# q and k loaded by token parity, so that one transpose takes two heads and one copy takes 128 partitions; epsilons added from a constant tile

## The chip, the cores and the metric

The kernel runs on 1 core of one Trainium2 chip. The metric is the device time of one execution in microseconds (us). Engines are called by the profile's names: PE (matrix multiply), PEld (its weight loads), DVE (vector), ACT (scalar), POOL (GpSimd), SP (the queue that issues nearly all DMAs here).

## What is computed

Three layers follow each other. Only the first one is touched by the layout part of the change; the epsilons stand in the first and the second.

```python
def _attn_ref(q, k, v):               # 4 batches, 8 heads, 576 tokens, 64 dims; chunks of 64 tokens
    scores = scale * np.matmul(q_c, k_c.transpose(0, 1, 2, 4, 3))
    scores = scores - np.max(scores, axis=-1, keepdims=True)
    attn = np.exp(scores)
    attn = attn / (np.sum(attn, axis=-1, keepdims=True) + 1e-09)
    out = np.matmul(attn, v_c)
...
def _moe_ref(x, w_gate, w1, w2):      # x: 2304 tokens x 512; 8 experts, 1024 hidden
    logits = x @ w_gate
    P = np.exp(logits - logits.max())
    for _ in range(8):
        P /= P.sum(1, keepdims=True) + 1e-09
        P /= P.sum(0, keepdims=True) + 1e-09
        P *= N / E
    for e in range(E):
        h = np.maximum(x @ w1[e], 0.0)
        out += P[:, e:e + 1] * (h @ w2[e])
...
def _moe2_ref(x, w_in, w_out, g_ln):  # SoLU, layer norm and a second product, 512 -> 1024 -> 512
```

All tensors are float32.

## The kernel before

**Stages.** The attention fills the first 110 us or so. Then come the expert products (split into high and low parts and arranged as a seven-product block scheme), which fill most of the time, with the eight Sinkhorn rounds (`sink_rows`, `sink_cols`) beside the first of them. The last layer stands at the end.

**The attention loop.** The 2304 tokens are cut into 18 tiles of 128 tokens (two chunks). The main loop runs over steps `s` and is software-pipelined by hand: at step `s` the program writes, in this order, the loads of the q and k that steps `s+4` and `s+5` transpose (`load_qk`, every second step), the load of v for tile `s-2` (`load_v`, four DMAs), the exponentials and sums of tile `s-3` (`attn_exp`), the product with v of tile `s-6` (`attn_pv`), the transposes of the probabilities of tile `s-5` (`attn_pt`), the scores of tile `s-2` (`attn_qk`) and the transposes of q or k (`attn_t(s)`: q at even steps, k at odd ones; one q and one k tile serve two tiles of tokens). Behind these, queues of small pieces of work are drained (`side`, `w_side`): splitting the attention's output into high and low parts (`x_hi` on ACT, `x_lo` mostly on POOL) and preparing expert weights (`w_steps`, on POOL and ACT). Each engine works its instructions off in the order in which they are written, so a wait on one instruction holds all that is behind it on that engine.

**DMAs.** SP issues the loads and the stores in program order. A DMA also waits until the DMA eight places ahead of it has landed. v of tile `s-2` is loaded at step `s` and read at step `s+4`. q, k and the prepared weights share one pool of 18 buffers, v and the weights' sums another of 6.

**The transposes of q and k (`attn_t`).** A row of the loaded q tile is a pair of neighbouring tokens of one head, so 128 partitions hold 128 pairs of tokens, and a row has 4 heads x 128 numbers (token 0's 64 dims, then token 1's). One 128x128 transpose thus takes one head with both tokens: the result in PSUM has the even tokens in the upper 64 partitions and the odd ones in the lower 64. The tile wanted, `qkt`, has two heads in its 128 partitions and the tokens in order. So each of the two PSUM banks (one for the even heads, one for the odd heads) is copied out in two pieces of 64 partitions:

```python
if t == 0 or (h and not i):
    nc.scalar.activation(out=to, in_=of, func=AF.Copy)
else:
    nc.vector.tensor_copy(to, of)
```

That is four copies of 64x512 for each tile: three on ACT and one on DVE for q, two on each for k. There are 9 q tiles and 9 k tiles.

**The epsilons.** In `attn_exp` (18 times), `sink_rows` (8) and `sink_cols` (8) the epsilon is added to a row of sums by a DVE `tensor_scalar` with an immediate.

Of the kernel before, what the change touches and what calls it, by code (L numbers as in the profile page):

```python
# [9 lines left out]
F32 = mybir.dt.float32  # L10
F32R = mybir.dt.float32r
U32 = mybir.dt.uint32
AF = mybir.ActivationFunctionType
ALU = mybir.AluOpType
# [30 lines left out]
def chunk_attention_sinkhorn_moe_solu_kernel(  # L45
# [13 lines left out]
    nc = tc.nc  # L59
    P = 128  # L60
    B, H, S, D = q.shape
    N, DM = out.shape
    E = w_gate.shape[1]
    F = w1.shape[2]
    NT = N // P
    KD = DM // P
    NP = H // 2
# [4 lines left out]
    EPS = 1e-9  # L72
# [18 lines left out]
    def unit(m):  # L91
        p, i = divmod(m, NU)
        return p, ORDER[p][i]
# [3 lines left out]
    for m in range(NM):  # L97
        p, u = unit(m)
# [4 lines left out]
    const = ctx.enter_context(tc.tile_pool(name="const", bufs=1))  # L103
# [6 lines left out]
    def bank(name):  # L110
        return ps.tile([P, 512], F32, tag="r", name=name)
# [11 lines left out]
    def four(shape, dt, name):  # L123
        return work.tile(shape, dt, tag="four", bufs=4, name=name)
# [10 lines left out]
    def wtile(shape, dt, name):  # L135
        return work.tile(shape, dt, tag="w", bufs=18, name=name)

    ident = const.tile([P, P], F32, name="ident")
    ones = const.tile([P, P], F32, name="ones")
    mhalf = const.tile([P, 1], F32, name="mhalf")  # L140
    g_sb = const.tile([P, KF], F32, name="g_sb")
    wg_raw = const.tile([P, KD, E], F32, name="wg_raw")

# [10 lines left out]
    qk, vs = {}, {}  # L154

    def load_qk(g):

        for i, src in enumerate((q, k)):
            qk[g, i] = [wtile([P, NP, 2 * D], F32, f"{'qk'[i]}{g}_{x}") for x in range(2)]
            done = 0  # L160
            while done < P:
                b, s = divmod(g * P + done, S // 2)
                n = min(P - done, S // 2 - s)
                for x in range(2):
                    nc.sync.dma_start(
                        out=qk[g, i][x][done:done + n],
                        in_=src[b, x * NP:(x + 1) * NP, 2 * s:2 * (s + n), :].rearrange(
                            "h (p t) d -> p h (t d)", t=2
                        ),
                    )  # L170
                done += n
# [13 lines left out]
    def attn_t(s):  # L185


        g, i = divmod(s, 2)
        a = qk.pop((g, i))
        qkt[g, i] = four([P, NP, 4, 64], F32, f"{'qk'[i]}t{g}")  # L190
        o = qkt[g, i].rearrange("p a c (x t) -> p a c t x", t=2)
        for h in range(2):
            pqk = bank(f"pqk{s}_{h}")
            for n in range(NP):
                x, y = divmod(2 * n + h, NP)
                nc.tensor.transpose(pqk[:, n * P:(n + 1) * P], a[x][:, y, :], ident)
            for t in range(2):
                to = o[h * 64:(h + 1) * 64, :, :, t, :]
                of = pqk[t * 64:(t + 1) * 64].rearrange("p (a c x) -> p a c x", a=NP, c=4)
                if t == 0 or (h and not i):  # L200
                    nc.scalar.activation(out=to, in_=of, func=AF.Copy)
                else:
                    nc.vector.tensor_copy(to, of)  # L203

    def attn_qk(t):

# [29 lines left out]
    def attn_exp(t):  # L236
        p, sm = attn[t]
        flat = p.rearrange("p a h x -> p (a h x)")
        heads = p.rearrange("p a h x -> p (a h) x")
        nc.scalar.activation(out=flat, in_=flat, func=AF.Exp, scale=SCALE)  # L240
        nc.vector.tensor_reduce(out=sm, in_=heads, axis=AX.X, op=ALU.add)
        nc.vector.tensor_scalar(out=sm, in0=sm, scalar1=EPS, scalar2=None, op0=ALU.add)
        nc.vector.reciprocal(out=sm, in_=sm)
        nc.gpsimd.tensor_tensor(
            out=heads, in0=heads, in1=sm.unsqueeze(2).to_broadcast([P, H, 64]), op=ALU.mult
        )
# [151 lines left out]
    def sink_rows():  # L398
        r = small.tile([P, NT], F32, tag="sr", name="sr")
        nc.vector.tensor_reduce(out=r, in_=pw, axis=AX.X, op=ALU.add)  # L400
        nc.vector.tensor_scalar(out=r, in0=r, scalar1=EPS, scalar2=None, op0=ALU.add)
        nc.vector.reciprocal(out=r, in_=r)
        nc.vector.tensor_tensor(
            out=pw, in0=pw, in1=r.unsqueeze(2).to_broadcast([P, NT, E]), op=ALU.mult
        )
# [8 lines left out]
    def sink_cols(pc):  # L414
        r = small.tile([P, E], F32, tag="sc", name="sc")
        nc.vector.tensor_reduce(
            out=r, in_=pc[:, :NT * E].rearrange("p (t e) -> p e t", e=E), axis=AX.X, op=ALU.add
        )
        nc.vector.tensor_scalar(out=r, in0=r, scalar1=EPS, scalar2=None, op0=ALU.add)
        nc.vector.reciprocal(out=r, in_=r)  # L420
        nc.vector.scalar_tensor_tensor(
            out=pw,
            in0=pw,
            scalar=float(N) / E,
            in1=r.unsqueeze(1).to_broadcast([P, NT, E]),
            op0=ALU.mult,
            op1=ALU.mult,
        )
# [88 lines left out]
    def w_steps(u):  # L517

        s = {}
        ts = nc.gpsimd.tensor_tensor  # L520

        def a(i, kh):
            return raws[u, 0][kh].rearrange("p (k i f) -> p k i f", k=2, i=2)[:, :, i, :]

        def tmp(n):
            i = ("S1", "S2", "S3", "S4").index(n)
            if i % 2 == 0:
                s["t", i // 2] = vtile([P, 2, 2, P], F32, f"ws{u}_{i}")
            s[n] = s["t", i // 2][:, i % 2]
            return s[n]  # L530

        def put(n, src):
            t = wtile([P, 2, 2, P], F32R, f"w{u}_{n}")
            split(t[:, 0], t[:, 1], src, nc.gpsimd)
            wo[u, n] = t
            i = WOPS.index(n)
            nc.sync.dma_start(
                out=w_kept[u][:, i * 512:(i + 1) * 512],
                in_=t.bitcast(F32).rearrange("p s k f -> p (s k f)"),
            )  # L540

        def s12():
            ts(out=tmp("S1"), in0=a(1, 0), in1=a(1, 1), op=ALU.add)
            ts(out=tmp("S2"), in0=s["S1"], in1=a(0, 0), op=ALU.subtract)

        def s34():
            ts(out=tmp("S3"), in0=a(0, 0), in1=a(1, 0), op=ALU.subtract)
            ts(out=tmp("S4"), in0=a(0, 1), in1=s["S2"], op=ALU.subtract)

        return [  # L550
            s12,
            lambda: put("A11", a(0, 0)),
            s34,
            lambda: put("A12", a(0, 1)),
            lambda: put("S2", s["S2"]),
            lambda: put("S3", s["S3"]),
            lambda: put("S1", s["S1"]),
            lambda: put("A22", a(1, 1)),
            lambda: put("S4", s["S4"]),
        ]  # L560
# [10 lines left out]
    def second_blocks(u):  # L571

        def block(n):
            def go():
                t = wtile([P, 2, 256], F32R, f"w2_{u}_{n}")
                split(t[:, 0], t[:, 1], w2_block(u, n), nc.gpsimd)
                wo2[u, n] = t
                if n != "A21" or u in PLAIN:
                    w_keep(u, n, True, t)
            return go  # L580

        return [block(n) for n in ("A11", "A12", "A21", "A22")]
# [508 lines left out]
    with tc.manual_schedule():  # L1091
# [4 lines left out]
            nc.tensor.transpose(warm[:, :P], ident, ident)  # L1096
        nc.gpsimd.memset(ones, 1.0)
        nc.gpsimd.memset(mhalf, -0.5)
        nc.gpsimd.memset(wg.bitcast(F32), 0.0)

        def split_gate():
# [41 lines left out]
        for g in range(AHEAD // 2):  # L1143
            load_qk(g)
        w_side.extend(w_steps(0))
        banks.clear()
        for s in range(NT + 6):
            if s % 2 == 0 and s + AHEAD < NT:
                load_qk((s + AHEAD) // 2)
# [15 lines left out]
            if s == NT:  # L1165
                a, b = w_steps(1), second_blocks(0)
                w_side.extend(a[:4] + b[:2] + a[4:7] + b[2:] + a[7:])
            if 0 <= s - 3 < NT:
                attn_exp(s - 3)
            if 0 <= s - 6 < NT:  # L1170
                attn_pv(s - 6)
                hp, r = divmod(s - 6, TH)
# [6 lines left out]
            if s < NT:  # L1179
                attn_t(s)  # L1180
# [25 lines left out]
        for m in range(NU, M2):  # L1206
# [3 lines left out]
            g = 7 * (NU + 2) + 6 * (m - NU)  # L1210
            event(g, lambda u=u: load_raw(u, (1,)))
            f = second_sums(u, nc.gpsimd, nc.gpsimd)
# [15 lines left out]
        for n in range(NM):  # L1228
            p, u = divmod(n, NU)
# [21 lines left out]
            if n < NU and n in EARLY:  # L1251
                f = second_sums(n, nc.vector, nc.vector)
# [46 lines left out]
        g = 7 * NM  # L1299
# [60 lines left out]
```

## Time and profile before

| what | value |
|---|---|
| timed runs | 1817.41 us median of 3 (1814.68 to 1820.43) |
| profiled execution | its span from the first to the last instruction is 1814.0 us; the page gives no other time of it, and the fastest timed run is 0.7 us longer, the median 3.4 us |
| PE busy | 1761.4 us, 97% of the span |
| PEld busy | 1701.2 us, 94% |
| DVE busy | 1474.2 us, 81% |
| POOL busy | 1050.4 us, 58% |
| ACT busy | 612.5 us, 34% |
| DMA | 313443 packets, 476.21 MB, mean 263 GB/s |

PE is nearly full over the whole span, but not at its start: in 40 slices of 45 us its busy tenths read 7 7 7 9 9 9 and so on, and those of DVE 6 9 5 8 9 9. The first three slices hold the attention and the start of the Sinkhorn rounds. A difference between two kernels that both have a full PE later shows in when that full stretch begins.

### The profile page before, as it was taken

Reading aid. Unit: us, or ns where it says so; the run is one execution under the profiler, and the core shown is the slowest. Engines: PE = TensorE matmul, PEld = TensorE weight load, DVE = VectorE, ACT = ScalarE, POOL = GpSimd, SP = SyncE. Lnnn points to the kernel's source line nnn. Section 1 sums busy time; section 2 is a strip of 40 time slices with the busy share of each in tenths; the row PEclk is TensorE's granted clock in tenths of the full one; section 3 lists DMA queues with packets and bytes.
Section 4 is the critical chain, followed back from the end, with each engine's and each line's share of the span. In section 5 each row is a group of like instructions: output and inputs, shape, how many; then the busy total and the mean of one; then the engine's idle time right before and its main releaser. Section 6 shows DMA issues by size and latency. Waiting matters only on the chain.

```text
span 1814.0 us, 31893 instructions
## 1 busy us (share of the span) xinstructions
PE 1761.4 (97%) x10827; PEld 1701.2 (94%) x10827; DVE 1474.2 (81%) x2264; ACT 612.5 (34%) x1368; POOL 1050.4 (58%) x1111
## 2 busy tenths in 40 slices
PE   7779999999999999999999999999999999999999
PEld 6668999999999999999999999999999999988887
DVE  6958899999889877778888888988888877766664
ACT  6843444444444312222222222222222322222222
POOL 2866799999988415455466665666565665400000
PEclk8999999999999999999999999999999999999999
DMA  7684888988878898998988889888888878931110
GB/s 186 187 289 155 305 280 293 334 317 289 316 288 309 317 352 263 342 350 317 326 301 277 301 282 385 293 279 276 283 286 285 272 256 272 299 139 64 56 47 30
DMA packets 313443, 476.21 MB, mean 263 GB/s; under 512 B 47664, under 2 KB 116416, under 8 KB 313280
## 3 DMA queue, kind: packets, MB, share of 16 engines
q1 hardware_dynamic: 312848, 471.80, 76.1%
q8 instruction: 87, 1.43, 0.3%
q10 hardware_dynamic: 432, 2.36, 0.3%
q14 instruction: 76, 0.62, 0.1%
HBM read 323.51 MB, written 150.54 MB: 261 GB/s over the span
## 4 chain that ended last, share of the span: by engine, by line
PE 84%; DVE 8%; DMA 5%; ACT 1%; issue 1%; POOL 0%; SPq 0%; DVEq 0%; ACTq 0%
PE y L803 20%; PE y L854 17%; PE Y L663 15%; PE X L663 10%; PE Z L663 10%; PE po L1077 5%; PE mh L1020 5%; DMA wl_A<-wk 2%; PE lt L1065 1%; DVE acc L830 1%; DMA wl_S<-wk 1%; DMA x_B<-xk_B 1%; DVE kt L203 1%; DMA xk_B<-x_B 1%; DMA v<-in_v_dram 0%
## 5 line engine op out<-in xcount | busy, mean ns | idle before, releaser
L683 POOL TENSOR_TENSOR ho_T<-hT,ho_T 128x384 fp32r<-128x384 f32 x188 | 211.1, 1124 | 175.9 <-ACT ho_T L682 168.4
L803 PE MATMUL y<-h,w_A 128*128 128x384 f32 x1536 | 304.8, 336 | 1.9 <-DVE acc L830 1.9
L803 PEld LDWEIGHTS y<-h,w_A 128*128 128x128 f32 x1536 | 269.6, 188 | 3.8 <-issue 2.5
L151 POOL TENSOR_TENSOR w_A<-raw,w_A 128x256 fp32r<-128x256 f32 x224 | 190.7, 864 | 73.6 <-ACT w_A L150 61.5
L758 DVE TENSOR_TENSOR t<-Y,s 128x384 f32<-128x384 f32 x192 | 106.1, 553 | 109.2 <-PE Y L663 92.6
L830 DVE TENSOR_TENSOR acc<-y,acc 128x768 f32<-128x768 f32 (+1 forms) x192 | 175.7, 915 | 10.7 <-PE y L803 9.9
L854 PE MATMUL y<-ho_T,wl_S 128*128 128x384 f32 x864 | 173.4, 335 | 0.2 <-DMA wl_S<-wk 0.2
L874 DVE TENSOR_TENSOR acc<-y,acc 128x768 f32<-128x768 f32 (+1 forms) x165 | 150.5, 915 | 17.8 <-PE y L854 17.7
L803 PE MATMUL y<-h,wl_A 128*128 128x384 f32 x768 | 153.3, 337 | 2.0 <-DMA wl_A<-wk 2.0
L663 PE MATMUL X<-x_B,wl_A 128*128 128x384 f32 x768 | 153.7, 334 | 0.0
L663 PE MATMUL Y<-x_T,wl_S 128*128 128x384 f32 x768 | 153.7, 334 | 0.0
L854 PEld LDWEIGHTS y<-ho_T,wl_S 128*128 128x128 f32 x864 | 152.5, 189 | 1.1 <-PE Z L663 0.5
L737 ACT ACTIVATE h<-c 128x384 fp32r<-128x384 f32 x132 | 69.3, 525 | 235.2 <-DVE c L733 226.6
L803 PEld LDWEIGHTS y<-h,wl_A 128*128 128x128 f32 x768 | 136.2, 190 | 2.8 <-ACT h L737 2.6
L682 ACT ACTIVATE ho_B<-c 128x384 fp32r<-128x384 f32 x96 | 50.5, 526 | 252.1 <-DVE c L716 215.4
L663 PEld LDWEIGHTS Y<-x_T,wl_S 128*128 128x128 f32 x768 | 135.0, 188 | 0.0
L663 PEld LDWEIGHTS X<-x_B,wl_A 128*128 128x128 f32 x768 | 135.0, 188 | 0.0
L682 ACT ACTIVATE ho_T<-hT 128x384 fp32r<-128x384 f32 x192 | 98.9, 516 | 105.1 <-POOL hT L691 100.3
L1051 POOL TENSOR_TENSOR r<-r,mhalf 128x1 f32<-128x1 f32 x18 | 9.9, 548 | 208.8 <-DVE r L1048 208.8
L758 DVE TENSOR_TENSOR c<-Z,t 128x384 f32<-128x384 f32 x192 | 105.1, 548 | 21.6 <-PE Z L663 13.8
L151 POOL TENSOR_TENSOR w_S<-ws,w_S 128x256 fp32r<-128x256 f32 x128 | 110.6, 881 | 7.6 <-ACT w_S L150 7.3
L854 PE MATMUL y<-ho_B,wl_A 128*128 128x384 f32 x576 | 114.8, 334 | 0.0
(172 smaller groups left out, 3877.3 us busy)
## 6 DMA issues: line engine op xcount, KB each, us to landing
wl_S<-wk SPq DMA_DIRECT2D x448, 256.0 KB, 5.2
wl_A<-wk SPq DMA_DIRECT2D x400, 256.0 KB, 5.2
wk<-w_S SPq DMA_DIRECT2D x256, 256.0 KB, 5.1
wk<-w_A SPq DMA_DIRECT2D x208, 256.0 KB, 4.5
raw<-in_moe_w_dram SPq DMA_DIRECT2D x77, 512.0 KB, 5.8
sh<-spread SPq DMA_DIRECT2D x64, 192.0 KB, 8.1
kept<-wp SPq DMA_DIRECT2D x32, 256.0 KB, 5.1
xk_T<-x_T SPq DMA_DIRECT2D x8, 768.0 KB, 4.8
```

Source lines behind the costliest of these rows:

```text
L151: (eng or nc.vector).tensor_tensor(out=lo, in0=src, in1=hi.bitcast(F32), op=ALU.subtract)
L663: nc.tensor.matmul(b, w[:, a, kk, :], x[:, c, kk, :], start=(first and kk == 0 and n == 0), stop=(kk == 1 and n == 2), skip_group_check=no ...
L682: nc.scalar.activation(out=hi, in_=x, func=AF.Copy)
L683: f = lambda: eng.tensor_tensor(out=lo, in0=x, in1=hi.bitcast(F32), op=ALU.subtract)
L737: nc.scalar.activation(out=hi, in_=hp, func=AF.Copy)
L758: nc.vector.tensor_tensor(out=c_of[n], in0=bank_, in1=c_of[other], op=ALU.add)
L803: nc.tensor.matmul(y, wo2[u, f"A{d // 2 + 1}{f + 1}"][:, a, i * P:(i + 1) * P], h[:, c, f, :], start=(f == 0 and n == 0), stop=(f == 1 and ...
L830: nc.vector.tensor_tensor(out=at, in0=y, in1=at, op=ALU.add)
L854: nc.tensor.matmul(y, wo2[unit(m + q_)[1], wn][:, a, i * P:(i + 1) * P], hop[m // 2, bn][:, q_, c, :], start=(q_ == 0 and o == 0), stop=(q ...
L874: nc.vector.tensor_tensor(out=at, in0=y, in1=at, op=ALU.add)
L1020: nc.tensor.matmul(ph[:, n * 512:(n + 1) * 512], x[a][:, kk, :], m_in[kk, c][:, n * 512:(n + 1) * 512], start=(kk == 0 and i == 0), stop=( ...
L1077: nc.tensor.matmul(po[t], lt[f // 4][a][:, f % 4, :], m_out[f, c], start=(f == 0 and i == 0), stop=(f == KF - 1 and i == 2),)
```

## The change

Three things are changed.

- `load_qk` lays q and k out as parity, head, dim in each partition (`[P, 2, NP, D]`) where it was head, parity, dim. The bytes are the same; the piece that lies in one run in DRAM and in the tile is now 64 numbers (256 bytes) long where it was 128 (512 bytes). The number of DMAs is the same.
- `attn_t` transposes two neighbouring heads of one parity at a time. The result has the two heads in the 128 partitions already, so each of the two banks (now one for each parity) is copied out by one instruction of 128x512: two on ACT for q, one on ACT and one on DVE for k. The number and size of the transposes are the same.
- The 34 epsilons of attention and Sinkhorn are added by a DVE `tensor_tensor` with a constant tile `eps` that POOL fills once at the start. The line in the last layer (`mlp_n`) stays as it was.

```diff
+    eps = const.tile([P, NT], F32, name="eps")
...
-            qk[g, i] = [wtile([P, NP, 2 * D], F32, f"{'qk'[i]}{g}_{x}") for x in range(2)]
+            qk[g, i] = [wtile([P, 2, NP, D], F32, f"{'qk'[i]}{g}_{x}") for x in range(2)]
...
                         in_=src[b, x * NP:(x + 1) * NP, 2 * s:2 * (s + n), :].rearrange(
-                            "h (p t) d -> p h (t d)", t=2
+                            "h (p t) d -> p t h d", t=2
...
-        for h in range(2):
-            pqk = bank(f"pqk{s}_{h}")
+        for t in range(2):
+            pqk = bank(f"pqk{s}_{t}")
             for n in range(NP):
-                x, y = divmod(2 * n + h, NP)
-                nc.tensor.transpose(pqk[:, n * P:(n + 1) * P], a[x][:, y, :], ident)
-            for t in range(2):
-                to = o[h * 64:(h + 1) * 64, :, :, t, :]
-                of = pqk[t * 64:(t + 1) * 64].rearrange("p (a c x) -> p a c x", a=NP, c=4)
-                if t == 0 or (h and not i):
-                    nc.scalar.activation(out=to, in_=of, func=AF.Copy)
-                else:
-                    nc.vector.tensor_copy(to, of)
+                x, y = divmod(2 * n, NP)
+                nc.tensor.transpose(
+                    pqk[:, n * P:(n + 1) * P],
+                    a[x][:, t, y:y + 2, :].rearrange("p h d -> p (h d)"),
+                    ident,
+                )
+            of = pqk.rearrange("p (a c x) -> p a c x", a=NP, c=4)
+            if t and i:
+                nc.vector.tensor_copy(o[:, :, :, t, :], of)
+            else:
+                nc.scalar.activation(out=o[:, :, :, t, :], in_=of, func=AF.Copy)
...
-        nc.vector.tensor_scalar(out=sm, in0=sm, scalar1=EPS, scalar2=None, op0=ALU.add)
+        nc.vector.tensor_tensor(out=sm, in0=sm, in1=eps[:, :H], op=ALU.add)
...
-        nc.vector.tensor_scalar(out=r, in0=r, scalar1=EPS, scalar2=None, op0=ALU.add)
+        nc.vector.tensor_tensor(out=r, in0=r, in1=eps, op=ALU.add)
...
+        nc.gpsimd.memset(eps, EPS)
```

On DVE, the second and third steps of the attention read as follows before (`s` are the scores, `p` the probabilities, `mx` their maxima, `sm` their sums, `pqk` the PSUM banks of the transposes; the numbers are buffers):

```order
L228 TENSOR_TENSOR p_251<-s_234,mx_252 128x2x4x64
L203 COPY qt_256<-pqk_0_257 64x512
L241 TENSOR_REDUCE sm_253<-p_251 128x8
L242 TENSOR_SCALAR sm_253<-sm_253 128x8
L243 RECIPROCAL sm_253<-sm_253 128x8
L227 TENSOR_REDUCE mx_299<-s_281 128x8
L228 TENSOR_TENSOR p_298<-s_281,mx_299 128x2x4x64
L203 COPY kt_303<-pqk_0_304 64x512
L203 COPY kt_303<-pqk_1_311 64x512
```

After the change the same place has no copy of q, one copy of k, and the epsilon with two inputs:

```order
L231 TENSOR_TENSOR p_249<-s_232,mx_250 128x2x4x64
L244 TENSOR_REDUCE sm_251<-p_249 128x8
L245 TENSOR_TENSOR sm_251<-sm_251,eps 128x8
L246 RECIPROCAL sm_251<-sm_251 128x8
L230 TENSOR_REDUCE mx_295<-s_277 128x8
L231 TENSOR_TENSOR p_294<-s_277,mx_295 128x2x4x64
L204 COPY kt_299<-pqk_1_306 128x512
```

Nothing else changes its place on DVE; over the kernel 18 rows fewer stand there (2230 for 2248), and 9 rows fewer on ACT (1337 for 1346; two neighbouring copies of one bank share a row).

On SP, around the sixth load of q and k, before:

```order
L180 DMA v_381<-in_v_dram 64x4x64 x4
L165 DMA q_0_435<-in_q_dram 128x4x128
L165 DMA q_1_436<-in_q_dram 128x4x128
L165 DMA k_0_439<-in_k_dram 128x4x128
L165 DMA k_1_440<-in_k_dram 128x4x128
L180 DMA v_443<-in_v_dram 64x4x64 x4
L180 DMA v_517<-in_v_dram 64x4x64 x4
```

and after:

```order
L181 DMA v_373<-in_v_dram 64x4x64 x4
L166 DMA q_0_425<-in_q_dram 128x8x64
L166 DMA q_1_426<-in_q_dram 128x8x64
L166 DMA k_0_429<-in_k_dram 128x8x64
L166 DMA k_1_430<-in_k_dram 128x8x64
L181 DMA v_433<-in_v_dram 64x4x64 x4
L181 DMA v_505<-in_v_dram 64x4x64 x4
```

No DMA has moved; SP has 1676 rows in both. Each load of q and k is made of 8 runs of 64 numbers for each partition where it was 4 runs of 128.

## Rows read from the trace of the kernel before

**Rows 1.** Busy time in a window: PE, PEld, DVE, ACT, POOL; clock, DMA share, GB/s.

```profile
60.00:80.00 20.00, 13.62 (x300) 11.41 (x301) 19.07 (x29) 15.38 (x28) 19.92 (x15) 1.00 0.70 187
```

**Rows 2.** Groups by line to 220 us: busy us, mean ns, idle before.

```profile
L201 ACT ACTIVATE qt<-pqk 64x512 f32<-64x512 f32 x27 | 16.9, 625 | 16.2 <-PE pqk L196 15.9
L203 DVE COPY kt<-pqk 64x512 f32<-64x512 f32 x18 | 12.5, 694 | 2.4 <-ACT kt L201 1.9
L242 DVE TENSOR_SCALAR sm<-sm 128x8 f32<-128x8 f32 x18 | 11.0, 613 | 0.6
L256 ACT ACTIVATE pt<-pt 128x512 f32<-128x512 f32 x18 | 10.5, 582 | 0.0
```

**Rows 3.** Chain of work that ended last, steps 2 and 3: start, us, what.

```profile
13.89 0.63 ACT qt L201
...
18.54 0.71 DVE kt L203
```

**Rows 4.** SP's issues in order of time: start, us, line, DMA, count.

```profile
4.11 2.45 SPq L165 DMA_DIRECT2D k<-in_k_dram  x2
...
35.88 1.85 SPq L165 DMA_DIRECT2D q<-in_q_dram  x2
37.82 1.02 SPq L165 DMA_DIRECT2D k<-in_k_dram  x2
38.89 5.90 SPq L180 DMA_DIRECT2D v<-in_v_dram  x8
...
80.07 2.63 SPq L180 DMA_DIRECT2D v<-in_v_dram  x4
```

**Rows 5.** Chain of work that ended last, around 40 us.

```profile
40.19 5.26 DMA v<-in_v_dram
45.50 1.24 PE px L267 x28
```

**Rows 6.** PE in order of time, the product of the thirteenth tile.

```profile
86.09 1.15 PE L267 MATMUL px<-pt,v 64*64 64x64 f32 x32
```

**Rows 7.** SP's issues by line: duration ns min/median/max, first and last start; v's landing.

```profile
L165 SPq DMA_DIRECT2D k<-in_k_dram x2: 499/503/507, 1.8 to 2.3; - x2
L165 SPq DMA_DIRECT2D q<-in_q_dram x4: 614/614/616, 22.9 to 24.8; - x4
L180 SPq DMA_DIRECT2D v<-in_v_dram x72: 595/615/1638, 15.2 to 101.6; - x72
DMA to landing us min/median/max: 2.3/3.1/5.3
L1154 SPq DMA_DIRECT2D g_sb<-in_moe_g_ln_dram x1: 505/505/505, 19.7 to 19.7; - x1
```

**Rows 8.** DMA traffic from 7 to 9, 55 to 57 and 42.5 to 42.8 us.

```profile
DMA packets 1187, 0.59 MB, mean 295 GB/s; under 512 B 36, under 2 KB 1187, under 8 KB 1187
...
q1 hardware_dynamic: 805, 0.19, 43.1%
...
DMA packets 208, 0.05 MB, mean 174 GB/s; under 512 B 199, under 2 KB 208, under 8 KB 208
```

**Rows 9.** DVE and POOL in order of time, one epsilon.

```profile
57.92 1.31 DVE L242 TENSOR_SCALAR sm<-sm 128x8 f32<-128x8 f32 x1
...
55.61 3.59 POOL L301 TENSOR_TENSOR x_B<-xf,x_B 128x768 fp32r<-128x768 f32 x2 [1.28 <-ACT x_B L297]
```

**Rows 10.** DVE and POOL in order of time, a two-input operation of Sinkhorn.

```profile
131.61 0.56 DVE L421 SCALAR_TENSOR_TENSOR pw<-pw,sc 128x144 f32<-128x144 f32 x1
...
131.26 0.75 POOL L151 TENSOR_TENSOR w_A<-raw,w_A 128x256 fp32r<-128x256 f32 x1
```

**Rows 11.** Durations by line on DVE: ns min/median/max, first and last start.

```profile
L242 DVE TENSOR_SCALAR sm<-sm x18: 170/452/1658, 15.9 to 99.7; 128x8 f32<-128x8 f32 x18
...
L421 DVE SCALAR_TENSOR_TENSOR pw<-pw,sc x8: 307/414/562, 131.6 to 168.6; 128x144 f32<-128x144 f32 x8
L1043 DVE TENSOR_TENSOR r<-su x18: 158/159/163, 1603.6 to 1797.9; 128x1 f32<-128x1 f32 x18
```

More of the change, by code (lines that the diff above doesn't have):

```diff
@@ L418, in sink_cols @@
         )
-        nc.vector.tensor_scalar(out=r, in0=r, scalar1=EPS, scalar2=None, op0=ALU.add)
+        nc.vector.tensor_tensor(out=r, in0=r, in1=eps[:, :E], op=ALU.add)
         nc.vector.reciprocal(out=r, in_=r)
```

## Prediction

> **What bounds the kernel now.** I read the busy slices of the page first: PE is full from the fourth slice on, so all that can move lies in the first 110 us or so. A change there moves the end of the kernel one for one, because the expert products wait for the attention's output and then fill PE. Next I read the windows of that stretch. In a typical one of 20 us DVE is busy for 19.07 and POOL for 19.92, PE for only 13.62 [rows 1]: here DVE and POOL look like the bound. The groups by line say what fills DVE and ACT: a copy of 64x512 out of PSUM takes 0.694 us on DVE and 0.625 on ACT [rows 2]. The chain of waits shows both kinds on the path: after the last of ACT's q copies come the exponentials, and after the second of DVE's k copies the scores [rows 3].
>
> Read only so far, removing copies must pay. But the chain also goes through SP's queue. From 35.88 to 44.79 us the rows of SP join almost without gaps, 8.77 us of issuing in 8.91 us [rows 4]. SP isn't waiting for buffers there; it is late with the program. The cost shows at tile 4: one of its v loads is issued at 40.19, lands 5.26 us later, and the product with v starts at 45.50, as soon as it is there [rows 5]. At tile 12 the four loads of v are issued by 82.70 [rows 4]; with the median landing of 3.1 us [rows 7] they are there at 85.8, and the product starts at 86.09 [rows 6]. So the loads of v arrive just in time both early and late in the attention: SP's pace and the pace of DVE, ACT and POOL are nearly equal. The reader should see that the first two views name a bound and the queue's own rows name a second one right behind it.
>
> **The change, part by part.**
>
> *The copies.* Each of the 18 q and k tiles has two copies of 128x512 where it had four of 64x512. A copy's time goes with the numbers in a partition, not with the partitions: ACT's 128x512 copy from PSUM takes 0.582 [rows 2], and I take 0.625 for the new ones, because they write with the same step of two as the old. DVE loses two copies for each pair of tiles, one of q and one of k: 18 x 0.694 = 12.5 us of busy time. ACT loses two as well, one of each: 18 x 0.625 = 11.2 us. On the path of a pair of steps stand one of ACT's (0.63) and one of DVE's (0.71) [rows 3], 1.34 us; there are eight such pairs after the first, so 10.7 us are to be had if nothing else is late. What is late next is v. From tile 2 to tile 12 the product with v can't begin before v is there, and SP has no gaps out of which it could come sooner. I count as a gain in this stretch only the slack of tile 12, 86.09 - 85.8 = 0.3 us, and behind it, where v has more room, the one ACT copy that stands before the high parts at the last k tile, 0.6. Together 0.9 us gained; at the lower bound nothing, at the upper bound all 10.7.
>
> *The loads: issue.* The number of DMAs is the same, 48 of q and k. What SP needs for one of 8 runs of 64 the trace doesn't show. The nearest rows: 0.503 for 128 partitions of 4 runs (512 pieces), 0.505 for 128 partitions of 8 runs of one number (1024 pieces), 0.614 for 64 partitions of 4 runs of 512 bytes and 0.615 for the same with 256 bytes [rows 7]. Neither the number nor the size of the pieces shows in the price, so I take +0. The upper bound is double the price, as 1024 pieces are double 512: +0.5 on each of 48, 24 us. Nothing excludes a lower price, but no row shows one for 128 partitions, so the lower bound is 0.
>
> *The loads: transfer.* q and k are 9.4 MB, 18432 pieces of 512 bytes before and 36864 of 256 after. In the full stretch from 7 to 9 us 1187 pieces, nearly all of 512 bytes, took 16 engines 2 us: 27.0 ns for each [rows 8]. From 55 to 57 us only v's pieces of 256 bytes move, and 43.1% of 16 engines for 2 us over 805 pieces is 17.1 ns. In 0.3 us of full traffic at 42.5 us 208 pieces, nearly all of 256 bytes, went by: 23.1 ns [rows 8]. So two small pieces cost 34.2 to 46.2 ns where one large one cost 27.0; I take 34.2, from the row with the more pieces. The Trainium skill ("DMA: Bandwidth & Descriptors", Why small descriptors are slow) speaks against this layout too: it counts a fixed overhead of about 3 cycles for each piece beside one cycle for 32 bytes. An estimate from that page is 11 cycles for 256 bytes and 19 for 512, so 2 x 11 / 19, 16% more; the rows agree in direction and show 27% to 71%. By the page's figure the sum below would be +0.6 instead of +1.7.
>
> The first four pairs of tiles, 4 MB, need 8192 x 27.0 / 16 = 13.8 us before and 16384 x 17.1 / 16 = 17.5 after, +3.7. This is the stretch in which SP is held up by full queues (2.45 us for two issues of k at 4.11, for some 1.0 when nothing holds them) [rows 4, 7]. I let a third of it reach SP's place in the program, +1.2, with bounds of 0 and 3.7. Later, 1 MB comes in a burst every second step. The bursts of the fifth and the seventh pair are split into eight DMAs each; at 0.614 for one [rows 7] their issue takes 4.9 us, longer than the transfer's 4.4, and hides it. In the other three, of four DMAs of 128 partitions, 2.0 us of issuing meet 4.4 us of transfer where 3.5 were needed; I take half of the 0.9 for each, 0.45 x 3 = +1.4, bounds 0 and 2.8. So v is later by 2.6 at tile 12. The DMAs of the weights, which share the engines, find a mean load of 0.70 in this stretch [rows 1] and stay hidden.
>
> *The epsilons.* The 18 in the attention take 0.613 in the mean but 0.170 at the least [rows 2, 11]: 18 x 0.443 = 8.0 us of waiting inside the instruction. One row says for whom: it began at 57.92 and ended at 59.23, and POOL's operations of 55.61 ended at 59.20 [rows 9]. Would a two-input operation not wait? A row of Sinkhorn with two inputs in SBUF began at 131.61 and ended at 132.17, 0.56 us for work that takes 0.307 when free, and POOL's operation ended at 132.01 [rows 10, 11]. It waits in the same way. So I take the saving as 0 and the price of the free instruction as equal (0.159 for one number with two inputs, 0.170 for eight with one [rows 11]). The bounds are 8.0 us less, and 34 x 0.137 = 4.7 us more if each cost the 0.307. The Trainium skill ("SBUF — State Buffer", Who interferes with whom) has the same rule, that a DVE instruction with two SBUF inputs contends with a POOL instruction that reads SBUF; by it, too, nothing is won here, and the trace agrees. POOL's filling of `eps` lies at the start, before POOL has anything else to do: 0.
>
> *The sum.* +1.2 + 1.4 (v later) - 0.9 (copies) + 0 (issue) + 0 (epsilons) = +1.7 us. The profiled execution would go from a span of 1814.0 to 1815.7, and the median, which stands 3.4 us above that span, from 1817.4 to 1819.1. I say 1819.0.
>
> **The rivals.** What a measurement of this kernel can tell from no change is about 0.3%, 5.5 us.
>
> 1. *The copies are the bound and v is not.* For it: both copies stand in the chain, and DVE is 95% busy. Against: v that lands as it is needed. It decides if SP, with its program unchanged, issues v earlier than now. All 10.7 us are gained: 1806.7. Chance 0.14.
> 2. *SP's issue grows with the pieces.* For it: nothing in the prices of rows 7, but a pattern of this shape doesn't occur in them. Against: the load with 1024 pieces. SP's lag lands on v at once, so 28 of the 48 loads (those from the fifth pair on) count; at +0.3 each, 8.4 us: 1827 with the rest of the sum. It decides, past the 5.5 us, from +0.13 a load on. Chance 0.16.
> 3. *Small pieces cost 23.1 ns when traffic is full.* The first 4 MB take 23.7 us, +9.9, and the bursts 5.9 us for 3.5; a third and a half of it reach v, 3.3 + 3.6 = 6.9, less 0.9: 1823.4, and up to 1830 if all of the start reaches it. Chance 0.15, half of it past 5.5 us.
> 4. *The two-input epsilon doesn't wait.* Up to 8.0 us: 1809.4, or 1811 with v's lateness. Against: rows 10. In the stretch where the waits are longest POOL is full anyway [rows 1], so half is likelier, 1815. Chance 0.05.
>
> **How the numbers follow.** The forecast has 0.50, its own range is 1815 to 1822. Faster: 0.14 of rival 1 and 0.02 of rival 4, 0.16. Slower: rival 2, half of rival 3, and 0.02 of the forecast's own tail, 0.26. The same: 0.58. The range leaves out a little more than half of rival 1 and the far parts of rivals 2 and 3: 1808 to 1827.
>
> **What would show it.** Right: DVE and ACT lose about 12 and 11 us of busy time before 110 us, and PE's waits for copies turn into waits for v; SP's issues of q and k keep 0.5 and 0.6 us where nothing holds them; the epsilon rows keep a mean near 0.6 and still end with POOL's operations. Wrong: v's loads issued earlier than now at tile 4 or 12 (rival 1), a price of q's issue above 0.63 (rival 2), a median of the epsilons near 0.17 (rival 4), or a difference that arises after 130 us, where I expect none.

## Result and the profile after

The changed kernel takes 1828.22 us (median of 4 runs, 1827.19 to 1828.51) beside 1818.14 for the kernel before (4 runs, 1814.68 to 1820.43): a ratio of 1.0058 (1.0045 to 1.007). That is 10.5 us slower by the ratio; the two medians differ by 10.1. The forecast was 1819.0 and no measurable difference; the time lies 1.2 us above the range.

The page of the kernel after has this span, these busy times and these DMA packets:

```profile
span 1826.7 us, 31859 instructions
PE 1771.1 (97%) x10827; PEld 1709.8 (94%) x10827; DVE 1456.7 (80%) x2246; ACT 601.4 (33%) x1350; POOL 1049.4 (57%) x1112
DMA packets 331874, 476.20 MB, mean 261 GB/s; under 512 B 84528, under 2 KB 134848, under 8 KB 331712
```

DVE lost 17.5 us of busy time and ACT 11.1, so the copies went away as planned. The bytes are the same, but 18431 packets came on top. The groups by line of the copies and of the attention's epsilon (busy us, mean ns, then idle time before and its releaser):

```profile
L206 ACT ACTIVATE qt<-pqk 128x512 f32<-128x512 f32 x18 | 10.9, 630 | 17.8 <-PE pqk L197 17.7
L204 DVE COPY kt<-pqk 128x512 f32<-128x512 f32 x9 | 6.1, 683 | 9.6 <-PE pqk L197 9.6
L245 DVE TENSOR_TENSOR sm<-sm,eps 128x8 f32<-128x8 f32 x18 | 10.2, 565 | 0.7
```

A copy of 128 partitions takes what one of 64 took [rows 2]: 0.630 on ACT, 0.683 on DVE. The window that answers to [rows 1] (busy time of PE, PEld, DVE, ACT, POOL; clock, DMA share, GB/s):

```profile
60.00:80.00 20.00, 14.60 (x251) 12.22 (x250) 16.18 (x24) 12.10 (x22) 19.43 (x15) 0.83 0.66 162
```

DVE is down from 19.07 to 16.18 busy us and ACT from 15.38 to 12.10, but both got through fewer instructions too. They have room now, and the program runs later: something else holds it. SP's queue in order of time shows what (start, us, line, DMA, count), to be read against [rows 4]:

```profile
0.73 1.46 SPq L166 DMA_DIRECT2D q<-in_q_dram  x2
...
6.49 2.34 SPq L166 DMA_DIRECT2D k<-in_k_dram  x2
...
18.26 2.46 SPq L166 DMA_DIRECT2D k<-in_k_dram  x2
20.76 3.01 SPq L181 DMA_DIRECT2D v<-in_v_dram  x4
...
40.51 2.23 SPq L166 DMA_DIRECT2D q<-in_q_dram  x2
42.84 1.95 SPq L166 DMA_DIRECT2D k<-in_k_dram  x2
44.84 6.66 SPq L181 DMA_DIRECT2D v<-in_v_dram  x8
51.59 2.68 SPq L166 DMA_DIRECT2D q<-in_q_dram  x4
54.40 3.67 SPq L166 DMA_DIRECT2D k<-in_k_dram  x4
...
90.25 2.65 SPq L181 DMA_DIRECT2D v<-in_v_dram  x4
```

The same places in the kernel before, which were not shown above:

```profile
15.15 3.84 SPq L180 DMA_DIRECT2D v<-in_v_dram  x4
...
44.89 2.06 SPq L165 DMA_DIRECT2D q<-in_q_dram  x4
47.08 2.15 SPq L165 DMA_DIRECT2D k<-in_k_dram  x4
```

v of tile 0 is issued at 20.76 where it was 15.15 (+5.6), v of tile 4 at 44.84 for 38.89 (+6.0), v of tile 12 at 90.25 for 80.07 (+10.2). The loads of v kept their price; the loads of q and k in front of them got longer at the start and in the bursts (6.35 us for 4.21 in the seventh pair). The DMA traffic of the kernel after from 4 to 16 us, where the engines are full, gives the price of a piece:

```profile
DMA packets 9956, 2.51 MB, mean 209 GB/s; under 512 B 9955, under 2 KB 9955, under 8 KB 9955
```

That is 16 x 12 us over 9956 pieces, 19.3 ns for one of 256 bytes. The 27.0 ns of one of 512 bytes are from 7 to 9 us [rows 8]; the same two microseconds after the change read:

```profile
DMA packets 1725, 0.44 MB, mean 218 GB/s; under 512 B 1725, under 2 KB 1725, under 8 KB 1725
```

18.6 ns a piece, so two small ones take 37.1 ns there, 38% more than one large one. Over the whole start (2 to 16 us before, 7337 packets; 2 to 20 us after, 14319) the prices are 30.5 and 20.1 ns, 32% more. The Trainium skill ("DMA: Bandwidth & Descriptors", Why small descriptors are slow) has the direction right; the 16% estimated from its figures is too little here.

The waits until 120 us (us in total, times, longest), first before, then after:

```profile
PE s L214 <- DVE kt L203: 8.3, 14, 2.4
PE px L267 <- DMA v<-in_v_dram: 0.7, 1, 0.7
```

```profile
PE px L270 <- DMA v<-in_v_dram: 11.8, 11, 3.9
PE s L217 <- DVE kt L204: 0.9, 1, 0.9
```

The last product with v in PE's timeline before:

```profile
110.00 1.15 PE L267 MATMUL px<-pt,v 64*64 64x64 f32 x32
```

And after, the products of tile 12 and of the last tile:

```profile
95.26 0.50 PE L270 MATMUL px<-pt,v 64*64 64x64 f32 x4
...
97.39 1.23 PE L270 MATMUL px<-pt,v 64*64 64x64 f32 x28 [1.62 <-DMA v<-in_v_dram]
...
119.00 1.15 PE L270 MATMUL px<-pt,v 64*64 64x64 f32 x32
```

PE's wait for DVE's copies of k (8.3 us before) went down to 0.9, and its wait for v rose from 0.7 to 11.8: one wait took the other's place, and grew. Of tile 12's 32 products four run at 95.26 and the other 28, which wait for v, start at 97.39; before, all ran from 86.09 on [rows 6]. The last tile starts at 119.00 for 110.00. Durations by line (first and last start at the end of the times) show whether the difference arises there, for a Sinkhorn product and for the expert sums:

```profile
L412 PE MATMUL pc<-pw,ones x16: 286/324/391, 140.3 to 176.4; 128*128 128x144 f32 x16
L833 DVE TENSOR_TENSOR acc<-y,acc x192: 541/945/959, 157.8 to 907.9; 128x768 f32<-128x768 f32 x176, 128x384 f32<-128x384 f32 x16
```

The first Sinkhorn product stood at 130.1 before, 10.2 us earlier: all that the timed runs differ by is there by then. The last expert sum stood at 894.5, 13.4 us earlier; so some 2 to 3 us more of the two profiled spans' difference arise between 660 and 900 us. The kernel with the copies alone (below), which isn't late at all in the attention, has 2.0 us of that too (896.5), so I don't put it down to the change.

### The profile page after: what moved, and what is told of

Read it like the earlier page. It is cut to its first block, busy times and chain, and to the rows that moved or that the text cites. A ratio compares the mean times of both kernels' runs of the same rounds, so it can differ in the third digit from the quotient of the medians.

```text
span 1826.7 us, 31859 instructions
## 1 busy us (share of the span) xinstructions
PE 1771.1 (97%) x10827; PEld 1709.8 (94%) x10827; DVE 1456.7 (80%) x2246; ACT 601.4 (33%) x1350; POOL 1049.4 (57%) x1112
## 4 chain that ended last, share of the span: by engine, by line
PE 84%; DVE 7%; DMA 4%; SPq 2%; issue 1%; ACT 1%; POOL 1%; DVEq 0%; ACTq 0%
PE y L806 19%; PE y L857 18%; PE Y L666 15%; PE X L666 10%; PE Z L666 9%; PE po L1080 5%; PE mh L1023 5%; DMA wl_A<-wk 1%; SPq L166 1%; DMA v<-in_v_dram 1%; SPq L181 1%; PE lt L1068 1%; DVE acc L833 1%; PE px L270 1%; DMA kept<-wp 1%
## 5 line engine op out<-in xcount | busy, mean ns | idle before, releaser
L833 DVE TENSOR_TENSOR acc<-y,acc 128x768 f32<-128x768 f32 (+1 forms) x192 | 175.7, 915 | 11.0 <-PE y L806 10.2
L877 DVE TENSOR_TENSOR acc<-y,acc 128x768 f32<-128x768 f32 (+1 forms) x165 | 150.6, 916 | 17.6 <-PE y L857 17.5
```

The costliest lines, as they stand in the source:

```text
L833: nc.vector.tensor_tensor(out=at, in0=y, in1=at, op=ALU.add)
L877: nc.vector.tensor_tensor(out=at, in0=y, in1=at, op=ALU.add)
```

## The experiments

Ratios are to the kernel before run on the same chip, with the 95% interval; 0.1% is 1.8 us, and differences in us are worked out from the ratios. The first three take a part of the change alone; the others change what SP has to issue, or what waits for it.

### The loads alone

```diff
-            qk[g, i] = [wtile([P, NP, 2 * D], ...
+            qk[g, i] = [wtile([P, 2, NP, D], ...
-                            "h (p t) d -> p h (t d)", t=2
+                            "h (p t) d -> p t h d", t=2
...
```

The transposes follow the new layout; the four copies of 64x512 for each tile and the epsilons are those of before.

> q and k loaded by parity and transposed two heads at a time as in the changed kernel, but each bank copied out in two pieces of 64x512 and the epsilons as before. If SP's queue paces the attention, the loads alone make the loss and the copies win nothing behind them: 1828 us (1825 to 1834), and v of tile 12 is issued some 10 us later than before, from 90 us on. If the loss comes from the new copies or the epsilons, about 1818.

Measured: 1828.49 us, ratio 1.0056 (1.0037 to 1.0075). v of tile 4 is issued at 45.96, of tile 12 at 90.29. The loads carry the whole loss; with them, copies and epsilons make no difference to be seen (1.0058 with them, 1.0056 without). The loads come here with the transposes that read them; in the kernel after, those of q took PE 14.8 us for 12.4 before and those of k 10.9 in both. They were not run apart from the loads.

### The copies alone

```diff
-        for h in range(2):
+        for t in range(2):
-                x, y = divmod(2 * n + h, NP)
+                x, y = divmod(2 * n + t, NP)
-            for t in range(2):
-                to = o[h * 64:(h + 1) * 64, :, :, t, :]
-                of = pqk[t * 64:(t + 1) * 64].rearrange("p (a c x) -> p a c x", a=NP, c=4)
...
+            of = pqk.rearrange("p (a c x) -> p a c x", a=NP, c=4)
+            if t and i:
+                nc.vector.tensor_copy(o[:, :, :, t, :], of)
+            else:
+                nc.scalar.activation(out=o[:, :, :, t, :], in_=of, func=AF.Copy)
```

> Loads, transposes and epsilons as before (512-byte runs), but each bank copied out by one instruction of 128x512 as in the changed kernel. The scores are then of permuted numbers, since a bank holds one head's two parities and not two heads; the amount of work is the same. If v comes just in time in the kernel before, SP lets little of it through: 1814 to 1818 us, with PE's waits for v growing by several us. If the copies are the bound: 1807.

Measured: 1819.79 us, ratio 1.0007 (0.9993 to 1.002). DVE's copies of k went from 18 to 9, and the waits of PE until 125 us have changed their kind, not their end:

```profile
PE px L265 <- DMA v<-in_v_dram: 6.0, 7, 2.6
```

v of tile 12 is issued at 80.11, as before. So rival 1 of the prediction falls: 18 copies on DVE and 18 on ACT are saved, and nothing is gained, because SP issues v no sooner.

### The epsilons alone

```diff
+    eps = const.tile([P, NT], F32, name="eps")
-        nc.vector.tensor_scalar(out=sm, in0=sm, scalar1=EPS, scalar2=None, op0=ALU.add)
+        nc.vector.tensor_tensor(out=sm, in0=sm, in1=eps[:, :H], op=ALU.add)
```

> The kernel before with the 34 epsilons added by a two-input operation from a constant tile, nothing else. If that operation waits for POOL as the one with an immediate does: 1818 us (1816 to 1820), with a mean near 0.6 us for the 18 of the attention. If it doesn't wait: their mean is near 0.17, and the time 1810 to 1815.

Measured: 1819.76 us, ratio 1.0004 (0.9989 to 1.0018). The group by line:

```profile
L243 DVE TENSOR_TENSOR sm<-sm,eps 128x8 f32<-128x8 f32 x18 | 11.1, 618 | 0.7
```

0.618 in the mean for 0.613 before [rows 2]: the two-input form waits as the other did. The Trainium skill ("SBUF — State Buffer", Who interferes with whom) says the same of a DVE instruction with two SBUF inputs beside a POOL instruction that reads SBUF, and the trace agrees.

### Half of v's loads on ACT's queue

```diff
-                nc.sync.dma_start(out=vs[t][h * 64:(h + 1) * 64, c], in_=src[h])
+                (nc.scalar if h else nc.sync).dma_start(
+                    out=vs[t][h * 64:(h + 1) * 64, c], in_=src[h]
+                )
```

(in the changed kernel)

> The changed kernel, with every second load of v (36 of 72) issued from ACT's queue. If the issue on SP is the pace, 36 x 0.615 = 22 us leave it, v is in time, and what the copies save shows: 1805 to 1815 us. If the transfer of the small pieces by the 16 engines is the pace, the loads are as late as in the changed kernel: 1825 or more. ACT's waits at the start of a load could take back some us.

Measured: 1834.15 us, ratio 1.0092 (1.0064 to 1.0119): the theory missed. ACT in order of time, with the idle time ahead of a row in brackets:

```profile
17.71 3.48 ACTq L181 DMA_DIRECT2D v<-in_v_dram  x2
21.24 0.63 ACT L245 ACTIVATE p<-p 128x512 f32<-128x512 f32 x1 [6.72 <-DMA v<-in_v_dram]
```

Two issues held ACT for 3.48 us while the start's loads filled the engines, and ahead of the exponential behind them ACT did no work for 6.72, those 3.48 among it. The queue that issues also has to be free to wait; ACT isn't. So this run tells nothing about how much SP was relieved, and the next ones change SP's work without using another engine.

### SP's pace: twice as many issues for the same pieces

```diff
-                    nc.sync.dma_start(
-                        out=qk[g, i][x][done:done + n],
-                        in_=src[b, x * NP:(x + 1) * NP, 2 * s:2 * (s + n), :].rearrange(
+                    for y in range(2):
+                        h0 = x * NP + y * 2
+                        nc.sync.dma_start(
+                            out=qk[g, i][x][done:done + n, y * 2:y * 2 + 2],
+                            in_=src[b, h0:h0 + 2, 2 * s:2 * (s + n), :].rearrange(
...
```

(in the kernel before)

> The kernel before, with each load of q and k cut into two of half the heads: 96 DMAs in place of 48, the same 512-byte pieces, bytes and order. Theory (SP's issuing paces the attention): the first four pairs are held up by the transfer anyway, but 28 of the added issues come behind them, at some 0.5 us each: v of tile 12 is issued up to 14 us later than 80.07, the product with v waits for v, and the time is 1825 to 1833. Rival (the loss of the changed kernel lies in the transfer of small pieces alone, and SP has room): within 0.3% of the kernel before, 1813 to 1823.

Measured: 1837.6 us, ratio 1.0105 (1.009 to 1.012), 19.1 us slower. SP's price of these loads, and v of tile 12 in its timeline:

```profile
L167 SPq DMA_DIRECT2D q<-in_q_dram x48: 395/467/1482, 0.7 to 87.4; - x48
```

```profile
98.82 2.64 SPq L182 DMA_DIRECT2D v<-in_v_dram  x4
```

v of tile 12 is 18.75 us later than before and the kernel 19.1. Pieces, bytes and order are untouched, so the pace of SP's issues alone moves the end, one for one. The expectation was too low because the start's 40 issues, 20.7 us, proved too many to be hidden behind the transfer (v of tile 0 at 21.75).

### The start and the rest apart

The layout, transposes and copies of after are used only from the fifth pair on (shown), or, with `g >= 4` in place of `g < 4`, only for the first four pairs:

```diff
-                            "h (p t) d -> p h (t d)", t=2
+                            "h (p t) d -> p h (t d)" if g < 4 else "h (p t) d -> p t h d", t=2
...
+        if g < 4:
+            for h in range(2):
+                pqk = bank(f"pqk{s}_{h}")
...
+            return
+        for t in range(2):
+            pqk = bank(f"pqk{s}_{t}")
```

> The first four pairs of q and k loaded, transposed and copied as before, the others (from the fifth pair on) as after; epsilons as before. Theory (the start and the later loads each cost SP about half of the 10 us): v of tile 0 is issued at 15.2 as before, v of tile 12 4 to 5 us later than 80.07, and the time is 1821 to 1825. Rival 1 (all is the start's 4 MB in small pieces, the rest follows from it): 1816 to 1820, v of tile 12 within 1 us of 80.07. Rival 2 (all is the price of the later loads): 1826 to 1829.

Measured: 1825.7 us, ratio 1.0042 (1.0028 to 1.0057), 7.6 us.

> The opposite mix: the first four pairs of q and k loaded, transposed and copied as after, the others as before; epsilons as before. Theory (halves): v of tile 0 is issued at 20.5 to 21, some 5.5 us later than before, the lateness is still 5 to 6 us at tile 12, since SP has no gap in which to make it good, and the time is 1822 to 1826. Rival 1 (all is the start): 1826 to 1829. Rival 2 (all is the price of the later loads; lateness at the start is made good by tile 12): 1816 to 1820.

Measured: 1822.29 us, ratio 1.0019 (1.0007 to 1.0032), 3.5 us. The issues of v of tile 0 and tile 12, first with the new layout from the fifth pair on, then with the new layout up to the fourth:

```profile
14.46 3.92 SPq L180 DMA_DIRECT2D v<-in_v_dram  x4
...
85.70 2.70 SPq L180 DMA_DIRECT2D v<-in_v_dram  x4
```

```profile
20.33 2.96 SPq L180 DMA_DIRECT2D v<-in_v_dram  x4
...
81.65 2.69 SPq L180 DMA_DIRECT2D v<-in_v_dram  x4
```

The two losses add up, 7.6 + 3.5 = 11.1 for 10.5 of the whole change. The later loads make v 5.6 us late at tile 12. The start makes it 5.2 us late at tile 0; at tile 12 SP has made good all but 1.6, but the kernel still loses 3.5. The two latenesses at tile 12 give only 7.2 of the 10.2 us, so these rows do not account for the adding up of the times. Neither "all in the start" nor "all later" holds; the larger part is later.

### v ahead of q and k in SP's program

```diff
+            if 0 <= s - 2 < NT:
+                load_v(s - 2)
             if s % 2 == 0 and s + AHEAD < NT:
                 load_qk((s + AHEAD) // 2)
-            if 0 <= s - 2 < NT:
-                load_v(s - 2)
```

(in the kernel before)

> The kernel before, with the four loads of v written ahead of the loads of q and k at even steps. If v's place in SP's program is what the product with v waits for, the even tiles' v comes 2 to 5 us sooner, and the time falls by 1 to 4 us: 1814 to 1817. If SP's rate and not the order is what counts, v of odd tiles and q and k keep their times and the time stays: 1817 to 1820. If q and k have no more slack than v, the scores wait for them instead: 1819 to 1823.

Measured: 1817.77 us, ratio 0.9996 (0.9982 to 1.0009): no change. v of tile 0 is issued at 12.12 for 15.15, that of tile 12 at 79.06 for 80.07, and PE waits 10.4 us for DVE's copies of k (8.3 before). An earlier v alone gains nothing: the copies are a limit as well.

### Half the issues

One DMA of all 8 heads in place of two of 4; in the kernel before, there with the copies of after, and in the kernel after:

```diff
-            qk[g, i] = [wtile([P, NP, 2 * D], F32, f"{'qk'[i]}{g}_{x}") for x in range(2)]
+            qk[g, i] = six([P, H, 2 * D], F32, f"{'qk'[i]}{g}")
-                for x in range(2):
-                    nc.sync.dma_start(
-                        out=qk[g, i][x][done:done + n],
-                        in_=src[b, x * NP:(x + 1) * NP, 2 * s:2 * (s + n), :].rearrange(
+                nc.sync.dma_start(
+                    out=qk[g, i][done:done + n],
+                    in_=src[b, :, 2 * s:2 * (s + n), :].rearrange(
...
```

> The kernel before, with one load of all 8 heads of q (and of k) in place of two of 4: 24 DMAs for 48, the same pieces of 512 bytes; the tiles come from the pool of the larger tiles. Theory (SP's rate, counted in issues): the first four pairs stay limited by the transfer, the 14 fewer issues behind them free 14 x 0.5 = 7 us of SP, v of tile 12 is issued before 76; but DVE's copies of k are next, so the time falls by 2 to 6 us: 1812 to 1816. Rival (an issue's price goes with its pieces, some 1.0 us for a load of 1024): SP wins nothing, 1816 to 1820.

Measured: 1817.76 us, ratio 1.0002 (0.9988 to 1.0016). SP and PE's wait:

```profile
33.80 0.60 SPq L164 DMA_DIRECT2D q<-in_q_dram  x1
...
74.41 2.66 SPq L179 DMA_DIRECT2D v<-in_v_dram  x4
```

```profile
PE s L212 <- DVE kt L201: 9.8, 14, 3.4
```

v of tile 12 is issued 5.7 us sooner, no product with v waits for it any more, and the time is the same: PE waits for DVE's copies of k instead.

> The one load of 8 heads of the kernel before (pieces of 512 bytes) with the copies of 128x512 of the changed kernel; heads and parities are mixed up in the scores, so that the output is of other numbers. Theory (the copies gained nothing because SP's rate came right behind them): with SP relieved they pay, 5 to 9 us, 1809 to 1813. Rival 1 (a load's price goes with its pieces, SP is not relieved): 1816 to 1821. Rival 2 (the copies would gain nothing even with v early, POOL or something else is the bound): the time of the kernel with one load and the old copies, within 2 us.

Measured: 1813.69 us, ratio 0.9984 (0.9972 to 0.9997). The last product with v in PE's timeline:

```profile
108.26 1.15 PE L263 MATMUL px<-pt,v 64*64 64x64 f32 x32
```

It starts at 108.26, where one load alone had it at 111.09 and the kernel before at 110.00. Less than expected, and the interval overlaps a little with that of one load alone (1.0002, from 0.9988); but of all the kernels run it is the only one whose interval lies under the kernel before, if closely. The copies seem to pay a little, once SP is out of their way; of either step alone these runs show no gain.

> The changed kernel with one load of all 8 heads of q (and of k) in place of two of 4: 24 DMAs, pieces of 256 bytes. If the price of a small-piece load is one of its number of DMAs, the later loads cost SP 14 x 0.65 in place of 28 x 0.65, v of tile 12 is issued near 84, and the time is 1818 to 1823, with the start's 3 to 4 us still in it. If the price goes with the pieces (2048 in one load, twice 0.65 or the drain at 1.1 for 1024), nothing changes against the changed kernel: 1826 to 1830.

Measured: 1827.38 us, ratio 1.0058 (1.0037 to 1.0079): as the changed kernel. SP's rows between 63 and 71 us:

```profile
63.17 0.62 SPq L165 DMA_DIRECT2D q<-in_q_dram  x1
63.84 1.64 SPq L165 DMA_DIRECT2D k<-in_k_dram  x1
65.57 5.51 SPq L180 DMA_DIRECT2D v<-in_v_dram  x4
```

The first load of the burst, 2048 small pieces, costs SP 0.62, as a load of half the pieces does, so the price of an issue doesn't go with its pieces. The second one takes 1.64, and the four of v behind them 5.51 where they take 2.5 to 2.6 when nothing holds them. What SP saved in issues it gave back waiting. The time of SP in the issues of q, k and v, summed over all rows of its timeline until 125 us (q and k of the first four pairs, those behind, the 72 of v), compares the kernels, one trace each:

| kernel | q, k of four pairs | q, k behind | v | sum | against before | time against before |
|---|---|---|---|---|---|---|
| before | 14.05 | 18.98 | 51.80 | 84.8 | | |
| after | 19.68 | 24.39 | 53.50 | 97.6 | +12.7 | +10.5 |
| twice the issues | 20.66 | 33.80 | 51.12 | 105.6 | +20.8 | +19.1 |
| new layout from the fifth pair | 13.38 | 23.60 | 57.75 | 94.7 | +9.9 | +7.6 |
| new layout for four pairs | 19.25 | 15.86 | 53.02 | 88.1 | +3.3 | +3.5 |
| one load, before | 11.77 | 9.15 | 60.80 | 81.7 | -3.1 | +0.4 |
| one load, after | 18.81 | 16.41 | 60.00 | 95.2 | +10.4 | +10.5 |

From 84.8 upwards the times of these kernels follow the sum; below it, they don't. Others follow it less well: the loads alone have a sum of 99.9 (+15.1) for +10.2 us, v written first 87.6 (+2.7) for -0.7. A difference of 2 us in one column can be chance: the loads behind the fourth pair, unchanged, took 16.85 in the kernel with the epsilons alone and 18.98 before. The issue of v of tile 12 is the closer sign of a loss: +10.2 in the kernel after and with the loads alone, +10.1 with one load after, +18.75 with twice the issues. Half the issues in the kernel after took 24.39 - 16.41 = 8.0 us from the later loads of q and k, and 60.00 - 53.50 = 6.5 of it came back in v.

### Away from DVE: q's last copy on ACT

```diff
-                if t == 0 or (h and not i):
+                if t == 0 or not i:
```

(in the kernel before with one load)

> The kernel before with one load of 8 heads of q (and of k), and q's one copy of DVE (64x512) moved to ACT, so that DVE has only k's two: what can be had of the copies without small pieces. With v early, PE waits 9.8 us for DVE's copies of k in the kernel with one load. Theory (SP's rate and DVE's copies are two limits close behind each other, and both are eased here): 9 x 0.695 = 6.3 us leave DVE, ACT takes 9 x 0.626 = 5.6 more, and the time falls by 1 to 4 us, 1813 to 1816. Rival 1 (DVE isn't the limit, the two k copies in a row are): the time of the kernel with one load, 1817 to 1819. Rival 2 (ACT's fourth copy holds back its k copies and exponentials): 1819 to 1823.

Measured: 1821.42 us, ratio 1.0022 (1.0012 to 1.0032). The waits until 125 us:

```profile
DVE sm L239 <- ACT p L238: 14.8, 10, 3.0
PE s L212 <- DVE kt L201: 11.3, 14, 4.4
```

A miss, with rival 2's result. DVE's wait for the exponentials rose from 5.8 to 14.8 us: q's fourth copy stands ahead of them on ACT. PE's wait for k's copies did not fall (9.8 before the shift). A copy moved is not a copy saved.

## Why the prediction was wrong, point by point

- **What bounds the kernel: right.** Two limits stand close behind each other, SP's pace and the copies. Twice the issues moved the end by 19.1 us, the copies alone by 1.3 (-1.3 to 3.6), one load alone by 0.4, both together by -2.9.
- **The copies, -0.9: right in kind.** DVE's 17.5 (12.5 forecast) and ACT's 11.1 us of busy time went away, and the ratio of the copies alone is 1.0007, since v came no sooner.
- **The epsilons, +0: right.** Means of 0.565 and 0.618 for 0.613, ratio 1.0004 for them alone.
- **Issue, "+0": a little too low, but the loss does not need it.** Where nothing holds them the new loads take SP 0.60 to 0.65 for 0.505 [rows 7]; on 28 loads that is at most 28 x 0.145 = 4.1 us. That is about the +0.13 from which rival 2 was to decide; yet halving the number of loads gave back almost all it saved (v of tile 12 at 90.16 for 90.25), so with small pieces the transfer alone is enough to hold SP in the later bursts.
- **Transfer, +1.2 and +1.4: the step that failed.** The mechanism was right (small pieces take longer, SP is held, v is late, the end moves); its size was not. The text has "I let a third of it reach SP's place" and "hides it" for the two split bursts. In fact all of the start reached SP: 16384 pieces x 19.3 ns / 16 = 19.8 us, and the last of their issues ends at 20.72; v of tile 0 was +5.6, not +1.2. At tile 12, where +2.6 was forecast, v was 10.2 us late. In the kernel's time the new layout at the start alone cost 3.5 us for +1.2, that of the later loads alone 7.6 for +1.4 (there with what their issue costs): the later bursts were the larger error. The price of 17.1 ns for a piece, from a stretch in which the engines were 43.1% busy, was the lower of the two rows, and 19.3 lies between them.
- **Hiding behind issues.** The prediction set 4.9 us of issuing beside 4.4 us of transfer in the split bursts and took the longer. The seventh pair's eight issues took 4.21 us before, not 4.9 (loads of 32 and 96 partitions are cheaper to issue than the 0.614 taken for them), and 6.35 after, so there nothing was left to hide the transfer. The fifth pair, split too, took 5.31 for 6.37, so the forecast of no loss held there (the old loads were held there too: 5.2 us where nothing holds them). The larger miss is in the three bursts that are not split: their issues of q and k took 12.73 us for 8.40, +4.3 for the +1.4 forecast. More than half of that is in the eighth pair, before and after:

```profile
56.24 1.15 SPq L165 DMA_DIRECT2D q<-in_q_dram  x2
57.44 1.06 SPq L165 DMA_DIRECT2D k<-in_k_dram  x2
```

```profile
64.16 1.35 SPq L166 DMA_DIRECT2D q<-in_q_dram  x2
65.56 3.37 SPq L166 DMA_DIRECT2D k<-in_k_dram  x2
```

The two loads of q cost 0.2 us more; the two of k behind them take 3.37 for 1.06.
- **Which rival came nearest.** Rival 3, small pieces at full traffic, whose end "up to 1830 if all of the start reaches it" is near the 1828.2 measured. That is partly luck: it put 9.9 us on the start and 3.6 on the later bursts, where the layout at the start alone cost 3.5 and that of the later loads alone 7.6.
- **What stays open.** How the 7.6 us of the later loads divide between issue price and transfer was not measured apart. An estimate from the rows of that kernel: at the least that they show for two and four loads (1.35 and 2.66 us) the later loads of q and k need 18.7 us for the 15.86 of old loads that nothing holds (the kernel with the new layout for four pairs); so 2.9 is issue price, and the other 4.9 of its 23.60 is holding, with more of it in v's rows. The 2 to 3 us between 660 and 900 us were not followed. SP's issues on another queue that has nothing to wait for were not tried.

## What to carry to other kernels

When a queue issues without gaps and its last loads land as they are needed, a microsecond that the queue is held can move the end (18.75 us at v and 19.1 at the end with twice the issues), and a share of it can't be discounted because "transfers overlap", not without rows that show the overlap. Before halving the run length of a load, price its pieces at full traffic and take the whole of the difference as the upper bound for the queue, then look at which of two near limits the saved work relieves: here neither of two eased limits alone showed a gain, and only both together gave 0.16%. And a DMA is issued best from a queue that has nothing else to do: an engine that computes is held by the issue as well.

## What the hardware showed that was not expected

- The price of an issue on SP hardly goes with its size. For one load: 0.467 us with two runs of 512 bytes in each partition (median of q's 48), 0.503 with four [rows 7], 0.60 with eight (33.80 us in the kernel with one load), 0.62 with sixteen of 256 bytes (63.17 us in the changed kernel with one load). Twice the number of loads therefore costs almost twice the time (33.80 us for 18.98 behind the fourth pair).
- The loads of 32 and 96 partitions in the seventh pair took 0.31 to 0.55 us each to issue before, for 0.614 with 64 partitions [rows 7]. With small pieces the four of q took 0.60 to 0.65 each (2.68 for the row at 51.59).
- PE's granted clock from 60 to 80 us was 0.83 after for 1.00 before [rows 1], while PE waited for v there. PE's busy time over the span rose by 9.7 us for the same work, 8.2 of it up to the last product with v (94.3 for 86.1), where PE waits anyway; so I count it as a consequence, without a run that shows it.
